# Transposing R, V and A with DMAs instead of TensorE, from the second chunk on, in a chunked recurrent-attention kernel

## The chip, the cores and the metric

The kernel runs on one core of one Trainium2 chip. The metric is the device time in microseconds (us). Three timed runs of the kernel before gave 332.66, 329.70 and 330.74 us; the median is 330.74. One execution was recorded by the hardware profiler.

## The reference

Six inputs r, k, v, w, a, b have the shape batch 4 x heads 8 x time 768 x head size 40. Each head keeps a 40 x 40 state and goes through time step by step; after that a two-layer network with a squared ReLU takes the result of all heads.

```python
for t in range(S):
    y[:, :, t] = np.einsum('bhd,bhde->bhe', rt, state)
    Sa = np.einsum('bhde,bhe->bhd', state, at)
    state_decay = state * wt[:, :, None, :] - np.einsum('bhd,bhe->bhde', Sa, bt)
    state = state_decay + np.einsum('bhd,bhe->bhde', vt, kt)
...
x = np.ascontiguousarray(attn_out.transpose(0, 2, 1, 3)).reshape(B * S, H * D)
h = x @ w_in
r = np.maximum(h, 0.0)
g = r * r
return (g @ w_out).astype(np.float32)
```

w_in is 320 x 2048 and w_out 2048 x 320; the output is 3072 x 320 in fp32.

## The kernel before

**Tiling.** Time is cut into 6 chunks of 128 steps (`L = 128`, `NCH = 6`). A unit called a batch in this document, `m` from 0 to 23, is one chunk of one batch element with all 8 heads: `m = 4 * chunk + batch element`. Within a chunk the recurrence is turned into matmuls over 128 x 128 tiles; from chunk to chunk a state (`UZ`, `UBD`) is carried. A stage `st` from 0 to 47 works on half a batch, 4 heads, so that 8 stages make a chunk; the main loop (L490) runs over the stages, with a little overhang.

**Loading.** `load(m)` (L75) issues six DMAs on the sync queue (SP), one each for W, K, B, A, V and R, of 160 KB; the tiles hold time on the partitions. Four batches may be loaded ahead. SP issues strictly in order. Beside the loads it carries `gather` (L405), eight small DMAs from SBUF to SBUF twice in a chunk that rearrange the result YS for the network, and the output rows (L460), two for each half chunk.

**Preparing a batch.** The steps are placed by a table (`when`, L470) at a stage and at one of several places, called lots, within the stage:

- `prep_cast` (L164), at stage 2m-4, lot 1: ScalarE takes the logarithm of W; GpSimd casts A, V and R to bf16 into padded tiles of 128 x 8 x 64 (two buffers each, by m % 2).
- `prep_decay` (L176), stage 2m-4, lot 4: a matmul makes the running sum of the logarithm, ScalarE the exponentials GI and G, GpSimd multiplies K and B.
- `prep_rv` (L199), stage 2m-3, lot 1: four transposes of R and four of V on TensorE (L197) into the PSUM tile t1, and one copy by ScalarE (L204) into the SBUF tile RV.
- `prep_kb` (L206), stage 2m-3, lot 4: the same for K and B.
- `prep_ga` (L214), stage 2m-2, lot 1: transposes of G and of A into the PSUM tile t3, a copy of G to GT by ScalarE (L224), and VectorE's product AT of A and GT (L225), which reads A from PSUM.
- `prep_load`, stage 2m-7, lot 5: the loads of batch m.

Each transpose handles two heads: 128 time rows by 2 x 64 columns. The tiles t1, t2, t3 share one PSUM tag of two buffers ("ff") with `cs` and with the tiles hp and op_ of the network.

**Stages.** A stage multiplies AT with KBT (`st_a_mm`, L235), masks it on VectorE (L250), goes through a short chain of corrections (P, Mc, c1, Sn: L252 to L300), transposes Sn (L310), multiplies RV (L332, which reads RV first at stage 2m+1), masks again (L349), and ends with uy (L353, L362) and YS and UZ (L373). Three pieces of the network's work (`filler`, L466) are put between the links of this chain in each stage, at the places where TensorE would otherwise sit still.

**Order.** The order is written out by hand and each engine works in program order; a wait at the head of an engine's queue holds all that is behind it. On SP each DMA also waits for the eighth DMA before it to land, because eight semaphores go round.

Of the kernel before, what the change touches and what calls it, by code (L numbers as in the profile page):

```python
# [8 lines left out]
BF16 = mybir.dt.bfloat16  # L9
I32 = mybir.dt.int32  # L10
ALU = mybir.AluOpType
# [7 lines left out]
def kernel(  # L19
# [21 lines left out]
    nc = tc.nc  # L41

    NB, NHH, T, D = r.shape
    L = 128
    NCH = T // L
    PB = NHH // 2
# [6 lines left out]
    LV = L + D  # L53
# [5 lines left out]
    gl = ctx.enter_context(tc.tile_pool(name="gl", bufs=1))  # L59
    chp = ctx.enter_context(tc.tile_pool(name="chp", bufs=2))  # L60
# [25 lines left out]
    for m in range(AHEAD):  # L86
# [11 lines left out]
        out=UTI[:], in_=ones_f[:], pattern=[[1, 128]],  # L98
# [7 lines left out]
        out=IDb[:], in_=ones_b[:], pattern=[[1, 128]],  # L106
# [3 lines left out]
    for i in range(30):  # L110
# [4 lines left out]
        out=MEX[:], in_=MEX[:], pattern=[[0, 4], [1, L]],  # L115
# [8 lines left out]
    for key, n in (("R", 2), ("V", 2), ("A", 2), ("G", 2), ("K", 4), ("B", 4)):  # L124
        pads[key] = []
        for i in range(n):
            t_ = gl.tile([128, NHH, 64], BF16, name=f"{key}p{i}")
# [3 lines left out]
    for i in range(4):  # L131
        t_ = gl.tile([128, PB, L + 2], BF16, name=f"GT{i}")
        nc.vector.memset(t_[:, :, 0:1], 1.0)
        GTs.append(t_)
        t_ = gl.tile([128, 2, PB, LV], BF16, name=f"RV{i}")
        nc.vector.memset(t_[:, :, :, L:LV], 0.0)
        for s in range(2):
            o_ = 64 * s
            nc.vector.tensor_copy(
                out=t_[o_:o_ + D, 0, :, L:LV],  # L140
                in_=IDb[o_:o_ + D, o_:o_ + D].rearrange("p (u d) -> p u d", u=1)
                .to_broadcast([D, PB, D]))
        RVs.append(t_)
    EVXs = []
    for i in range(NEV):
        t_ = gl.tile([128, 2, 2, EV], BF16, name=f"EVX{i}")
# [7 lines left out]
    def half(s):  # L154
        return slice(64 * s, 64 * s + 64)
# [3 lines left out]
    bt = {}  # L159
# [34 lines left out]
    def transposes(dst, pad):  # L194
        for j in range(PB):
            src = pad[:, 2 * j:2 * j + 2, :].rearrange("p a b -> p (a b)")
            nc.tensor.transpose(out=dst[:, j, :], in_=src, identity=IDb[:])  # L197

    def prep_rv(m):  # L199
        o = bt[m]  # L200
        t1 = ps.tile([128, 2, PB, L], BF16, name="t1", tag="ff", bufs=2)
        transposes(t1[:, 0], o.R)
        transposes(t1[:, 1], o.V)
        nc.scalar.activation(out=o.RV[:, :, :, 0:L], in_=t1[:], func=ACTF.Copy)  # L204
# [9 lines left out]
    def prep_ga(m):  # L214
        o = bt[m]
        for u in range(2):
            nc.gpsimd.tensor_copy(
                out=o.EVX[u][:, :, :, L:LV].rearrange("p i s e -> p (i s) e"),
                in_=o.V[:, 4 * u:4 * u + 4, 0:D])
        o.AT = chp.tile([128, PB, L], BF16, name="AT", tag="AT", bufs=3)  # L220
        t3 = ps.tile([128, 2, PB, L], BF16, name="t3", tag="ff", bufs=2)
        transposes(t3[:, 0], o.G)
        transposes(t3[:, 1], o.A)
        nc.scalar.activation(out=o.GT[:, :, 1:L + 1], in_=t3[:, 0], func=ACTF.Copy)  # L224
        nc.vector.tensor_tensor(out=o.AT[:], in0=t3[:, 1], in1=o.GT[:, :, 0:L], op=ALU.mult)  # L225

    def where(st):
        c, q = divmod(st, NQ)  # L230
        return c, bt[c * NB + q // 2], (q % 2) * 2, slice(2 * q, 2 * q + 2), EVXs[st % NEV]
# [3 lines left out]
    def st_a_mm(st):  # L235
        c, o, j0, p2, EVX = where(st)
        ca = CNs[st, "ps"] = [ps.tile([128, 2, 2, L], FP32, name=f"ca{s}", tag=f"ca{s}")
                              for s in range(2)]
        for u in range(2):
            for i in range(2):  # L240
                for s in range(2):
                    nc.tensor.matmul(out=ca[s][:, i, u, :], lhsT=o.KBT[half(s), u, j0 + i, :],  # L242
                                     rhs=o.AT[half(s), j0 + i, :], start=(i == 0 and u == 0),
                                     stop=True, skip_group_check=True)
# [65 lines left out]
    def st_t(st, su):  # L310
        tb = ps.tile([128, 4, 128], BF16, name="tb", tag="sp")
        if st < NS:
            EVX = EVXs[st % NEV]
            for i in range(2):
                for s in range(2):
                    nc.tensor.transpose(out=tb[half(s), i, :], in_=EVX[:, i, s, L + LV:EV],  # L316
                                        identity=IDb[:])
        if 0 <= su < NS - NQ:
            c, q = divmod(su, NQ)
            for i in range(2):  # L320
                for s in range(2):
                    nc.tensor.transpose(out=tb[half(s), 2 + i, :], identity=IDb[:],  # L322
                                        in_=UZs[(c + 1) % 2][:, 2 * q + i, half(s)])
        if st < NS:
            SnT = SnTs[st] = qdp.tile([128, 2, L], BF16, name="SnT", tag="SnT")
            nc.vector.tensor_copy(out=SnT[:], in_=tb[:, 0:2])  # L326
        if 0 <= su < NS - NQ:
            nc.scalar.activation(out=UBD[:, 2 * q:2 * q + 2, :], in_=tb[:, 2:4], func=ACTF.Copy)
# [3 lines left out]
    def st_ex_mm(st):  # L332
        c, o, j0, p2, EVX = where(st)
        SnT = SnTs.pop(st)
        ex = exs[st] = [ps.tile([128, 2, 2, L], FP32, name=f"ex{s}", tag=f"ex{s}")
                        for s in range(2)]
        for u in range(2):
            for i in range(2):
                for s in range(2):
                    lhsT = SnT[half(s), i, :] if u else o.RV[half(s), 1, j0 + i, 0:L]  # L340
                    nc.tensor.matmul(out=ex[s][:, i, u, :], lhsT=lhsT,  # L341
                                     rhs=o.RV[half(s), 0, j0 + i, 0:L],
                                     start=(i == 0 and u == 0), stop=True, skip_group_check=True)
# [9 lines left out]
    def st_z(st):  # L353
        c, o, j0, p2, EVX = where(st)
        uy = uys[st] = ps.tile([128, 2, LV], FP32, name="uy", tag="uy")
        if c > 0:
            for i in range(2):
                nc.tensor.matmul(out=uy[:, i, :], lhsT=UBD[:, p2.start + i, :],
                                 rhs=o.RV[:, 0, j0 + i, :], start=(i == 0), stop=False,
                                 skip_group_check=True)  # L360

    def st_kb(st):  # L362
# [39 lines left out]
    def load_wout():  # L402
        nc.gpsimd.dma_start(out=WOUT[:], in_=moe_w_out.rearrange("(j p) f -> p j f", p=128))
# [62 lines left out]
    def filler(st):  # L466
        if fill and fill[0][0] <= st:
            fill.pop(0)[1]()

    when = {}  # L470
    for m in range(1, NBC):
        for ds_, lot, f in ((-4, 1, prep_cast), (-4, 4, prep_decay), (-3, 1, prep_rv),
                            (-3, 4, prep_kb), (-2, 1, prep_ga), (-7, 5, prep_load)):
            if f is not prep_load or m >= AHEAD:
                when.setdefault((2 * m + ds_, lot), []).append((f, m))

    def prepare(st, lot):
        for f, m in when.pop((st, lot), []):
            f(m)
# [10 lines left out]
    for st in range(NS + 2):  # L490
        if 1 <= st <= NS:
            st_ex_mm(st - 1)
        if st + 1 < NS:
            st_a_mm(st + 1)
        filler(st)
        if st >= 2:
            st_y(st - 2)
        if 1 <= st <= NS:
            st_ex_ev(st - 1)
            st_z(st - 1)  # L500
        if st < NS:
            st_p(st)
            st_m(st)
        prepare(st, 1)
        if st < NS:
            st_corr(st, Mc[st // NQ][:, st % NQ], False)
            st_c1(st)
        if st + 1 < NS:
            st_a_ev(st + 1)
        filler(st)  # L510
        if st < NS:
            st_corr(st, c1s[st], True)
            st_sn(st)
        filler(st)
        prepare(st, 4)
        st_t(st, st - 2)
        if 1 <= st <= NS:
            st_kb(st - 1)
        if st == 1:
            load_win()  # L520
        if st == 4:
            load_wout()
        if st >= 2:
            c, q = divmod(st - 2, NQ)
            hf = q // (NQ // 2)
            if q % (NQ // 2) == NQ // 2 - 1:
                gather(c, hf, [nc.sync] if st < NS + 1 else [nc.sync, nc.gpsimd, nc.sync])
                at = st + (3 if c + 1 < NCH else 2)
                fill += [(at, lambda c=c, hf=hf, j=j: ffn_in(c, hf, j)) for j in range(NJ // 2)]
                fill += [(at, lambda c=c, hf=hf, b_=b_, p_=p_: ffn_out(c, hf, b_, p_))  # L530
                         for b_ in range(HB) for p_ in range(2)]
        prepare(st, 5)
        if st == 3:
            nc.gpsimd.memset(UZs[0][:], 0.0)
# [133 lines left out]
```

## Time and profile before

| what | value |
|---|---|
| median of three timed runs | 330.74 us (329.70 to 332.66) |
| the profiled execution's own time | 330.49 us |
| span of the profile, first to last instruction | 328.8 us |
| mean granted TensorE clock | 0.943 |
| ScalarE busy | 232.8 us (71%) |
| VectorE busy | 222.7 us (68%) |
| GpSimd busy | 188.3 us (57%) |
| transposes of R, V, A on TensorE (L197) | 96 each |
| copy of R and V out of PSUM (L204) | 24, mean 1023 ns |
| product AT (L225) | 24, mean 425 ns |

The span is what the instructions cover; the execution's own time lies 1.7 us above it. A row of a group gives busy time, mean duration of one, and the idle time ahead of it. The busy time of TensorE counts overlapping matmuls once, so that a matmul whose mean duration is 230 ns may add far less than that to it. The stages of the middle of the run are alike: a chunk takes 48.0 us (the same copy of the last Cc tile ends at 156.46, 204.43 and so on), so two batches take 24 us.

### The profile page before, as it was taken

The page shows a single profiled execution, that of the slowest core. Times are in us where ns is not written, and L with a number is a line of the kernel's source. Part 1 is how long each engine was busy: PE and PEld are TensorE (multiplying, and loading weights), DVE is VectorE, ACT ScalarE, POOL GpSimd, SP SyncE. Part 2 cuts the span into 40 slices and gives each one's busy share as a digit, 9 for nine tenths or more (in the row PEclk, how much of TensorE's full clock was granted, in tenths as well). Part 3 has the DMA queues.
Part 4 walks back from the last instruction along what each step waited for, and adds up shares of the span by engine and source line. Part 5 has one row for each costly group of instructions (what it writes and reads, how often), then busy time and mean ns, then how long its engine had stood idle before and what let it go on. Part 6 is the DMA issues. An engine that isn't in the chain of part 4 may idle for free.

```text
span 328.8 us, 10009 instructions
## 1 busy us (share of the span) xinstructions
PE 280.4 (85%) x3856; PEld 213.3 (65%) x3856; DVE 222.7 (68%) x545; ACT 232.8 (71%) x569; POOL 188.3 (57%) x342
## 2 busy tenths in 40 slices
PE   4478777799999799999799999899998899888990
PEld 3446555577777577777577777677776677666770
DVE  7226968587787587786686886686876775954430
ACT  3366766886886986887986787886887886538450
POOL 3367757296585485676476676476674673533300
PEclk9555978899999999999999999999999999999997
DMA  8992999985737437635736844735862701000100
GB/s 136 174 165 40 176 165 167 169 126 99 151 71 138 94 69 141 126 69 112 128 55 121 147 82 78 144 62 120 131 106 47 147 18 44 20 23 28 55 22 29
DMA packets 164187, 32.86 MB, mean 100 GB/s; under 512 B 158660, under 2 KB 163780, under 8 KB 164130
## 3 DMA queue, kind: packets, MB, share of 16 engines
q1 hardware_dynamic: 161586, 29.44, 49.7%
q0 software_dynamic: 2544, 2.68, 5.1%
q8 instruction: 32, 0.52, 0.7%
q14 instruction: 25, 0.20, 0.2%
HBM read 28.84 MB, written 3.93 MB: 100 GB/s over the span
## 4 chain that ended last, share of the span: by engine, by line
PE 56%; ACT 18%; issue 7%; DVE 7%; POOL 4%; DMA 3%; SPq 3%; ACTq 0%; DVEq 0%; POOLq 0%
PE hp L428 12%; PE t L197 6%; PE ex L341 4%; PE P L280 4%; PE cs L179 4%; ACT hs L433 3%; ACT jm L307 3%; PE uy L368 3%; ACT RV L204 3%; SPq L81 3%; PE tb L316 3%; PE ca L242 2%; DMA NV<-in_v_dram 2%; DVE c L288 2%; ACT GT L224 2%
## 5 line engine op out<-in xcount | busy, mean ns | idle before, releaser
L428 PE MATMUL hp<-X,WIN 120*128 120x256 bf16 (+1 forms) x576 | 78.9, 275 | 8.1 <-ACT osb L458 6.1
L433 ACT ACTIVATE hs<-hp 128x512 bf16<-128x512 f32 x96 | 57.3, 597 | 26.1 <-PE hp L428 22.7
L349 DVE TENSOR_TENSOR EVX<-ex,MEX 128x512 bf16<-128x512 f32 x96 | 61.8, 686 | 1.7 <-PE ex L341 0.5
L428 PEld LDWEIGHTS <-WIN 120*128 120x128 bf16 (+1 forms) x576 | 50.7, 98 | 18.9 <-issue 9.6
L250 DVE TENSOR_TENSOR CN<-ca,MCN 128x512 bf16<-128x512 f32 x96 | 61.4, 681 | 0.7 <-PE ca L242 0.7
L299 POOL TENSOR_TENSOR x<-Mc,c 128x160 f32<-128x160 bf16 x48 | 23.3, 486 | 66.7 <-DVE c L288 66.6
L436 POOL TENSOR_TENSOR Gt<-hs 128x512 bf16<-128x512 bf16 x43 | 48.4, 1125 | 9.9 <-ACT hs L433 9.6
L454 PEld LDWEIGHTS <-Gt 128*128 128x128 bf16 x384 | 34.3, 97 | 13.4 <-POOL Gt L436 0.8
L280 PEld LDWEIGHTS <-CN 128*128 128x128 bf16 x384 | 23.2, 98 | 27.2 <-issue 23.6
L326 DVE COPY SnT<-tb 128x256 bf16<-128x256 bf16 x48 | 14.0, 291 | 33.3 <-PE tb L322 27.6
L300 POOL TENSOR_TENSOR Cc<-x,EVX 128x160 bf16<-128x160 f32 x48 | 25.3, 527 | 17.1 <-ACT EVX L296 16.8
L436 DVE TENSOR_TENSOR Gt<-hs 128x512 bf16<-128x512 bf16 x53 | 27.4, 519 | 9.4 <-ACT hs L433 9.2
L225 DVE TENSOR_TENSOR AT<-t,GT 128x512 bf16<-128x512 bf16 x24 | 10.2, 425 | 31.4 <-ACT GT L224 31.4
L302 ACT ACTIVATE jk<-CN 128x512 bf16<-128x512 bf16 x48 | 30.1, 627 | 0.0
L212 ACT ACTIVATE KBT<-t 128x1024 bf16<-128x1024 bf16 x24 | 24.6, 1024 | 6.0 <-PE t L197 6.0
L204 ACT ACTIVATE RV<-t 128x1024 bf16<-128x1024 bf16 x24 | 24.6, 1023 | 5.1 <-PE t L197 3.0
L188 POOL TENSOR_TENSOR Kp<-NK,GI 128x320 bf16<-128x320 f32 x24 | 22.4, 933 | 6.6 <-ACT GI L182 5.6
L280 PE MATMUL P<-c,CN 128*128 128x40 bf16 x192 | 12.4, 181 | 13.5 <-DVE c L288 13.5
L288 DVE TENSOR_TENSOR c<-P,Mc 128x160 bf16<-128x160 f32 x48 | 15.3, 319 | 10.4 <-PE P L280 9.6
L378 DVE TENSOR_TENSOR YS<-uy,GT 128x256 bf16<-128x256 f32 x48 | 20.2, 421 | 1.2 <-PE uy L368 0.8
L242 PE MATMUL ca<-AT,KBT 64*128 64x128 bf16 x384 | 20.0, 228 | 1.2 <-DVE AT L225 1.2
L296 ACT ACTIVATE EVX<-P 128x160 bf16<-128x160 f32 x48 | 14.4, 300 | 8.7 <-PE P L280 8.4
(142 smaller groups left out, 636.6 us busy)
## 6 DMA issues: line engine op xcount, KB each, us to landing
NW<-in_w_dram SPq DMA_DIRECT2D x24, 160.0 KB
NK<-in_k_dram SPq DMA_DIRECT2D x24, 160.0 KB
NB<-in_b_dram SPq DMA_DIRECT2D x24, 160.0 KB
NA<-in_a_dram SPq DMA_DIRECT2D x24, 160.0 KB
NV<-in_v_dram SPq DMA_DIRECT2D x24, 160.0 KB
NR<-in_r_dram SPq DMA_DIRECT2D x24, 160.0 KB
out_dram<-osb SPq DMA_DIRECT2D x24, 160.0 KB
X<-YS SPq DMA_DIRECT2D x93, 20.0 KB
```

The lines of the kernel that those rows point to most:

```text
L204: nc.scalar.activation(out=o.RV[:, :, :, 0:L], in_=t1[:], func=ACTF.Copy)
L212: nc.scalar.activation(out=o.KBT[:], in_=t2[:], func=ACTF.Copy)
L242: nc.tensor.matmul(out=ca[s][:, i, u, :], lhsT=o.KBT[half(s), u, j0 + i, :], rhs=o.AT[half(s), j0 + i, :], start=(i == 0 and u == 0), stop ...
L250: nc.vector.tensor_tensor(out=CN[:, :, s], in0=ca[s][:], in1=MCN[:], op=ALU.mult)
L280: nc.tensor.matmul(out=P[:, i, s, 0:D], lhsT=CN[:, i, s, 1, :], rhs=X[:, 2 * i + s], start=False, stop=last, skip_group_check=True)
L300: nc.gpsimd.tensor_tensor(out=Cc[c][:, q], in0=t_[:], in1=Sn, op=ALU.add)
L302: nc.scalar.activation(out=jk[:], in_=CN[:, :, :, 1, :], func=ACTF.Square, accum_out=ACC[:, AN + st:AN + st + 1])
L349: nc.vector.tensor_tensor(out=EVX[:, :, s, 0:2 * LV].rearrange("p i (u x) -> p i u x", u=2)[:, :, :, 0:L], in0=ex[s][:], in1=MEX[:].rearra ...
L428: nc.tensor.matmul(out=hp[:, u, :], lhsT=WIN[g][0:rows[g], j * 128:(j + 1) * 128], rhs=Xs[c, hf][g][0:rows[g]].rearrange("p a b -> p (a b) ...
L433: nc.scalar.activation(out=hs[:], in_=hp[:].rearrange("p u x -> p (u x)"), func=ACTF.Relu)
L436: later.append(lambda: eng.tensor_tensor(out=Gt[:, 2 * jj:2 * jj + 2].rearrange("p j a b -> p (j a b)"), in0=hs[:], in1=hs[:], op=ALU.mult))
L454: nc.tensor.matmul(out=op_[:], lhsT=Gts[c, hf][:, j, b_, :], rhs=WOUT[:, j, :], start=(j == 0), stop=(j == NJ - 1))
```

## The change

From batch 4 on (`m >= NB`, the second chunk) the transposes of R, V and A on TensorE and the copy of R and V by ScalarE go. In their place `prep_turn` issues three transposing DMAs on the sync queue, for A, V and R in that order, each from a padded bf16 tile of 128 x 512 to an SBUF tile of 128 x 4 x 128. It stands at stage 2m-4 in a new lot 3, which is run after lot 4. A goes to a new tile AR with two buffers; V and R go straight into RV, whose rows become 8 elements longer. G, K and B are transposed on TensorE as before. The product AT reads A from AR, in SBUF. The first four batches stay as they were.

```diff
-        t_ = gl.tile([128, 2, PB, LV], BF16, name=f"RV{i}")
-        nc.vector.memset(t_[:, :, :, L:LV], 0.0)
+        t_ = gl.tile([128, 2, PB, LV + 8], BF16, name=f"RV{i}")
+        nc.vector.memset(t_[:, :, :, L:LV + 8], 0.0)
...
+    def by_dma(m):
+        return m >= NB
+
+    def prep_turn(m):
+        o = bt[m]
+        if by_dma(m):
+            o.AR = chp.tile([128, PB, L], BF16, name="AR", tag="AR")
+            for dst, pad in ((o.AR[:], o.A), (o.RV[:, 1], o.V), (o.RV[:, 0], o.R)):
+                nc.sync.dma_start_transpose(out=dst[:, :, 0:L],
+                                            in_=pad[:].rearrange("p h e -> p (h e)"))
+
     def prep_rv(m):
         o = bt[m]
+        if by_dma(m):
+            return
...
-        transposes(t3[:, 1], o.A)
+        if not by_dma(m):
+            transposes(t3[:, 1], o.A)
...
-        nc.vector.tensor_tensor(out=o.AT[:], in0=t3[:, 1], in1=o.GT[:, :, 0:L], op=ALU.mult)
+        nc.vector.tensor_tensor(out=o.AT[:], in0=o.AR[:] if by_dma(m) else t3[:, 1],
+                                in1=o.GT[:, :, 0:L], op=ALU.mult)
...
-                                 rhs=o.RV[:, 0, j0 + i, :], start=(i == 0), stop=False,
+                                 rhs=o.RV[:, 0, j0 + i, 0:LV], start=(i == 0), stop=False,
...
-        for ds_, lot, f in ((-4, 1, prep_cast), (-4, 4, prep_decay), (-3, 1, prep_rv),
+        for ds_, lot, f in ((-4, 1, prep_cast), (-4, 3, prep_turn), (-4, 4, prep_decay), (-3, 1, prep_rv),
...
         prepare(st, 4)
+        prepare(st, 3)
```

In the built program TensorE issues 240 transposes fewer (20 batches of 12, each with its weight load), ScalarE 20 copies fewer, and SP 60 DMAs more; no other engine's instructions change in number. On SP the order within two batches becomes: three transposes, two output rows, six loads, three transposes, eight gather DMAs, six loads.

## The prediction

> **What bounds the kernel now.** I read the page first, for how full each engine is, then the table by stretches, for where.
>
> ```profile
> PE 280.4 (85%) x3856; PEld 213.3 (65%) x3856; DVE 222.7 (68%) x545; ACT 232.8 (71%) x569; POOL 188.3 (57%) x342
> ```
>
> TensorE leads, but the shares are means over unlike stretches, so the table decides. Its columns: length, busy time of TensorE (PE), its weight loads, VectorE (DVE), ScalarE (ACT), GpSimd (POOL), granted clock, DMA share, GB/s.
>
> ```profile
> 20.00:62.00 42.00, 31.17 (x457) 22.91 (x455) 31.43 (x73) 29.65 (x74) 27.83 (x56) 0.78 0.86 142
> 158.00:206.00 48.00, 44.43 (x648) 34.04 (x648) 35.70 (x85) 38.52 (x98) 30.97 (x56) 1.00 0.58 105
> 254.00:300.00 46.00, 41.34 (x577) 31.16 (x577) 31.68 (x69) 31.73 (x79) 22.55 (x35) 1.00 0.21 45
> ```
>
> From 62 us on TensorE is 44.4 of 48 us busy at full granted clock: it bounds the chunk. Before that the DMA engines do (0.86). The chain of waits, 164 to 171 us (start, length, what), says the same with one addition: ScalarE's copy of R and V stands in it.
>
> ```profile
> 165.44 0.47 PE t L197 x8
> 165.91 0.02 issue
> 165.93 1.03 ACT RV L204
> 166.96 0.04 issue
> 167.00 0.82 PE hp L428 x6
> ```
>
> Eight transposes take 0.47 us there, and then TensorE's next product waits for the copy, since both use the PSUM tag "ff". Over 158 to 206 the chain gives PE t 6.7% and the copy 4.1%.
>
> The new work goes to the sync queue and the DMA engines. SP's timeline over one period of two batches:
>
> ```profile
> 158.10 0.36 SPq L460 DMA_DIRECT2D out_dram<-osb  x1
> 158.55 0.39 SPq L81 DMA_DIRECT2D NW<-in_w_dram  x1
> ...
> 162.12 0.63 SPq L81 DMA_DIRECT2D NR<-in_r_dram  x1
> 162.85 7.40 SPq L411 DMA_DIRECT2D X<-YS  x8
> 170.35 0.44 SPq L81 DMA_DIRECT2D NW<-in_w_dram  x1
> ...
> 174.52 0.89 SPq L81 DMA_DIRECT2D NR<-in_r_dram  x1
> 177.26 3.60 SPq L460 DMA_DIRECT2D out_dram<-osb  x2
> 180.96 0.40 SPq L81 DMA_DIRECT2D NW<-in_w_dram  x1
> ```
>
> SP is free only from 175.4 to 177.3, in the stretch of 3.6 us that holds two output rows, and between the two rows of the other half; it waits there for ScalarE's osb. The DMA queue over 158 to 206:
>
> ```profile
> q1 hardware_dynamic: 26976, 4.92, 57.3%
> ```
>
> So 57.3% x 24 = 13.75 us of all 16 engines go per two batches, and one packet takes 0.573 x 16 x 48 us / 26976 = 16.3 ns.
>
> **The change part by part.** The sum is made against the profiled execution, 330.5 us (span 328.8 and 1.7 around it), 0.2 below the median of 330.74.
>
> *TensorE's transposes go.* The line of the transposes alone, over the same stretch (PE, then weight loads):
>
> ```profile
> 158.00:206.00 48.00, 7.29 (x96) 5.76 (x96) 1.00 0.58 105
> ```
>
> That is 96 transposes a chunk, 76 ns each; R, V and A are half, so 3.65 us a chunk, 0.91 us a batch. *ScalarE's copy goes*: 20 x 1.02 = 20.5 us of its busy time, on the path in two of four batches (at 165.9 and at 189.1). Chain: half of PE t's 6.7% (1.6 us) and the copy's 4.1% (2.0 us) make 3.6 us a chunk. The two views agree; I take 0.91 us a batch. Of 20 batches the first two are prepared between 50 and 68 us, where the DMA share is 0.89 to 1.21, and give nothing: 18 x 0.91 = -16.4 us. Bounds: 0, if a chain of dependent work sets the stage; and 20 x (0.91 + 1.02) = -38.6, if every copy's time came back beside the transposes'.
>
> *Sixty DMAs on SP, issue.* No row shows a transposing DMA. Call its time on SP i. The nearest rows are the loads, 128 partitions like it, with medians of 0.44 to 0.84 us, and the gather, SBUF to SBUF like it, 0.77 us. I take 0.8. Lower bound 0.37 (the shortest load). Upper bound: a load moves 1024 packets; if the issue followed the number of pieces and a piece were 32 bytes (the instruction's unit is 16 rows by 128 columns, so 16 elements of 2 bytes land in a row), 131072 / 32 = 4096 pieces, 4 x 0.84 = 3.4 us. The queue's budget per two batches: loads 2 x 4.2 (158.55 to 162.75), gather 6.7, two rows 0.8, together 15.9; with 6 x 0.8 it is 20.7, and the new pace is 24 - 1.8 = 22.2. It fits, cost 0. It stops fitting at i = 1.05.
>
> *The same, on the DMA engines.* Call the time t. With 512 packets (128 partitions x 4 runs of 256 bytes) x 16.3 ns / 16 it is 0.52 us, with 4096 packets 4.2 us. I take 0.52, because the loads and gathers beside it are counted in whole runs too. 13.75 + 6 x 0.52 = 16.9 of 22.2 us: hidden. Where it isn't hidden is the DMA-bound stretch to 68 us: two batches, 6 x 0.52 = +3.1 us.
>
> A rule against the change: the Trainium skill, page "VectorE: DVE Perf Modes", section "The three transpose paths", gives 1309 ns for a 128x128 bf16 transpose by DMA and 390 ns by TensorE. The trace has 57 to 76 ns of TensorE's time apiece in the stream, and no DMA transpose. By the page, as an estimate, four in one DMA would hold the engines 5.2 us, and two batches would need 13.75 + 31.4 = 45 us: about 540 us in all. Its page "DMA: Bandwidth & Descriptors", section "Latency and other measured facts", gives 261 GB/s for transposing DMAs, 0.5 us for 128 KB, by which the sum stays as it is. No row of this trace shows which holds.
>
> *New waits.* SP's transposes wait for GpSimd's casts; the cast of R ends at 156.8 and at 171.6, and SP reaches them at 162.8 and after 175: nothing queues behind that. The buffers RV and AR were last read four and two batches earlier. Behind the transposes stand the gather and the loads. The gather ends 3i = 2.4 us later, lands 1.8 us after that (its three issues by GpSimd show 1.8), at 174.5; the first hp that reads it starts at 181.7. The second load, landing up to 4.1 us after issue (the DMA NV piece of the chain at 40.5), has the cast at 180.4 as reader: NR would land at 175.4 + 4.1 + 2.4 = 181.9 against its cast at 181.2. GpSimd idles up to 4.75 us behind the casts, which covers it; if that cover is gone, it costs 0.7 + 1.8 us per two batches, +25 us.
>
> AT is the tightest. It waits for AR, and behind it on VectorE stand c1 and the next masks, for which TensorE's corrections wait. SP reaches the second A at 162.75 + 3i + 6.7 + 5.1; issue i, landing 2.3 (1.8 + 0.52): 176.9 + 4i, 180.1 at 0.8. AT now starts at 183.9, at the new pace 181.9. So 1.8 us are left, none with a landing of 4.1.
>
> *Small edits.* AT read from SBUF: the products of two SBUF tiles of that size (Gt on VectorE) have a median of 456 ns, at least 415 and at most 1255, against 425: 20 x 0.03 = +0.6 us, -0.2 to +16.6; VectorE has 12 us free a chunk, 0. The longer RV: four memsets of 192 ns a fifth longer, in the first 7 us, beside the loads; 0. The sliced read has the same shape; 0.
>
> Sum: 330.5 - 16.4 + 3.1 = 317.2, stated as **317**.
>
> **The rivals.**
>
> *SP becomes the bound (slower).* Each 0.1 us of i beyond 1.05 costs 0.6 us per two batches; there are ten such periods, and some 6 us of lead between a landing and its reader are used up once. It eats the gain of 13.3 when 10 x (15.9 + 6i - 22.2) - 6 = 13.3, at i = 1.37. At i = 2 it gives 317 + 51 = 368 us, at 3.4 about 452. For it: SP is already busy 16 to 17 of 24 us, and the gather's 0.77 us for 20 KB shows that little data isn't a short issue. Against: no issue row has a median above 0.84.
>
> *The DMA engines become the bound (slower).* By the same sum with 13.75 + 6t they eat the gain at t = 1.73; at 4.2 it is about 475 us. [...] Against: 42% of the engines' time is free.
>
> *Hidden, and nothing gained.* If the stage's chain of P, c1, Sn, SnT sets the pace, the removed work was filler, and the time is 330.5 to 334. For it: waits such as SnT on PE tb (27.6 us in all). Against: TensorE's 44.4 of 48.
>
> *More than forecast.* If the freed "ff" buffer and ScalarE also count, up to 38.6 - 3.1 below: 295.
>
> That the change doesn't do what it says is excluded: the built program has the 240 transposes and 20 copies fewer.
>
> **How the numbers follow.** Chances: the forecast (308 to 327 as its own range: the gain from 22 down to 4) 0.45; SP the bound 0.27, because i is unmeasured and 1.05 is close to the rows (0.02 of it faster, 0.05 within 1%, 0.20 slower); the engines the bound 0.17 (0.01 within 1%, 0.16 slower); nothing gained 0.08 (0.06 and 0.02); more than forecast 0.03. Faster by over 1%, about what a measurement can tell here, 0.50; within 1% 0.12; slower 0.38. The range reaches from 308 to 368, SP's case at i = 2; about 0.05 lie below and 0.13 above.
>
> **What would show it.** Right: in 158 to 206, or its like, PE about 40.8 us a chunk, no RV row on ScalarE for later batches, a chunk of 44.4 us, SP issues of prep_turn near 0.8 us, VectorE's wait ahead of AT still ending on GT. Wrong: issues above 1.05 us and SP without gaps; AT or GpSimd's casts ended by a DMA; a DMA share near 1 past 68 us; or chunks of 48 us with PE at 40.8, which would be the chain.

## The result, and the profile after

The changed kernel takes 357.83 us (median of 4 runs, 356.40 to 361.17) against 331.05 us for the kernel before beside it: a ratio of 1.082, with a 95% interval of 1.073 to 1.091. It is slower by 8%. The forecast was 317, with 308 to 368 as the range: the time lies inside the range and on the other side of no change. The profiled execution took 361.17 us, the longest of the four, its span 359.4 us. Medians below are over all runs of a kernel; the ratios leave out the few runs that lie over 1.5% above the fastest of theirs.

First the line of busy times on the page of the kernel after, and the chain that ended last, by engine and by line.

```profile
PE 278.2 (77%) x3616; PEld 207.1 (58%) x3616; DVE 224.6 (62%) x545; ACT 215.3 (60%) x549; POOL 190.5 (53%) x342
...
PE 44%; DMA 16%; SPq 12%; issue 8%; ACT 8%; DVE 5%; POOL 4%; DVEq 0%; ACTq 0%; POOLq 0%
PE hp L443 13%; DMA AR<-Ap 12%; SPq L81 11%; PE cs L179 4%; PE P L295 4%; PE ex L356 3%; ACT hs L448 3%; PE uy L383 3%; DMA NW<-in_w_dram 3%; PE tb L331 2%; DVE c L303 2%; PE ca L257 2%; PE t L197 2%; ACT Mc L288 2%; ACT osb L473 1%
```

ScalarE lost its 17.5 us (232.8 to 215.3), as the change says. TensorE lost only 2.2 us of the 18 that 240 transposes of 76 ns make. The chain has a member that it did not have, the landing of the transposed A (12%), and one that has grown, the sync queue's issue of loads (11%, before 3%).

Two rows of the table by stretches, with the columns of the prediction's table, show the slower pace. The second has 493 matmuls where there were 648, and its granted clock, 1.00 before, is 0.97. The first has 0.88 (0.96 before), and the two stretches from 206 to 300 us have 0.89 (1.00 before).

```profile
62.00:110.00 48.00, 40.17 (x530) 30.05 (x529) 33.85 (x79) 32.73 (x84) 28.92 (x54) 0.88 0.76 128
158.00:206.00 48.00, 35.68 (x493) 26.82 (x493) 29.97 (x70) 29.93 (x79) 25.80 (x50) 0.97 0.67 113
```

TensorE now stands still for microseconds at a time, and in the stall read here it has a lower clock behind it:

```profile
204.58 0.29 PE L295 MATMUL P<-c,CN 128*128 128x40 bf16 x4 [4.38 <-DVE c L303]
```

In the single microseconds from 203 to 206 us the clock reads 0.57, 0.50 and 0.50, and it is still 0.50 up to 209 us. So a part of this stall is paid twice. For the whole run, the kernel of e9 below, which has the same matmuls, can be set beside it: TensorE is busy for 268.8 us there, at a mean clock of 0.931 against 0.892. So about 9 of the 278.2 us go with the stalls and the lower clock. That even e9 lost 11.6 us and not 18 is left open.

What the new instructions cost the sync queue is in the view of their line (shortest, median, longest duration in ns):

```profile
L207 SPq DMA_TRANSPOSE AR<-Ap x20: 1194/1394/1601, 48.3 to 303.9; - x20
L207 SPq DMA_TRANSPOSE RV<-Vp x20: 1189/1197/2325, 49.9 to 305.2; - x20
L207 SPq DMA_TRANSPOSE RV<-Rp x20: 1188/1206/2588, 51.2 to 307.6; - x20
```

None takes less than 1.19 us; I had taken 0.8. The timeline of SP over two batches of the kernel after:

```profile
177.21 1.00 SPq L475 DMA_DIRECT2D out_dram<-osb  x2
178.31 1.90 SPq L81 DMA_DIRECT2D NW<-in_w_dram  x1
...
184.07 1.47 SPq L207 DMA_TRANSPOSE AR<-Ap  x1
185.64 1.19 SPq L207 DMA_TRANSPOSE RV<-Vp  x1
186.94 1.74 SPq L207 DMA_TRANSPOSE RV<-Rp  x1
188.77 6.73 SPq L426 DMA_DIRECT2D X<-YS  x8
195.60 0.44 SPq L81 DMA_DIRECT2D NW<-in_w_dram  x1
...
198.73 2.13 SPq L81 DMA_DIRECT2D NR<-in_r_dram  x1
200.96 1.42 SPq L207 DMA_TRANSPOSE AR<-Ap  x1
...
205.08 1.00 SPq L475 DMA_DIRECT2D out_dram<-osb  x2
```

The pauses at the output rows are gone: the two rows take 1.00 us, where SP used to wait for ScalarE within 3.6 or 6.0 us. The queue is full. Over the five periods from 124.35 to 258.87 us a period of two batches takes 26.9 us: transposes 8.0, twelve loads 9.6, gather 6.7, rows 1.0, gaps between instructions 1.6. (The expectations below take 27.2.)

What the late queue does is in the chain of waits of the same stretch (start, length, what), and in the list of waits (total, times, longest):

```profile
184.07 3.42 DMA AR<-Ap
187.49 0.03 issue
187.52 0.02 DVEq L239
...
198.73 2.13 SPq L81
...
200.96 2.82 DMA AR<-Ap
```

```profile
POOL Ap L174 <- DMA NA<-in_a_dram: 44.4, 12, 6.0
...
DVE AT L239 <- DMA AR<-Ap: 37.2, 12, 5.4
```

The same in the kernel before:

```profile
DVE AT L225 <- ACT GT L224: 31.4, 24, 4.1
...
POOL Ap L174 <- DMA NA<-in_a_dram: 15.2, 4, 5.6
```

AT now waits for A's transpose, and GpSimd's casts, which the next transposes need, wait for loads that were issued late. Both are what the prediction named as tight places; each was passed.

Chunk periods are the best ruler for the experiments. Each is the distance between the starts of the last copies of Cc on ScalarE; the first number is the start of the first such copy, called the end of the first chunk here. All are in us, from one profiled execution each, and the first chunk is the least certain: in kernels without a wait for a transposed A there it ends between 58.5 and 61.4 us.

| kernel | first chunk ends | the five chunks after |
|---|---|---|
| before | 59.9 | 48.6, 48.0, 48.0, 48.0, 45.4 |
| after | 65.0 | 52.0, 53.1, 56.3, 52.0, 50.6 |
| e1 transposes beside | 60.2 | 57.7, 55.1, 52.6, 52.4, 48.9 |
| e2 V and R only | 59.9 | 50.3, 48.0, 48.6, 48.5, 45.6 |
| e3 A only | 66.1 | 47.4, 47.7, 47.7, 47.7, 45.1 |
| e5 no gather | 67.0 | 47.0, 47.5, 47.4, 47.4, 46.2 |
| e9 no transposes | 61.4 | 47.4, 47.5, 47.4, 47.5, 45.0 |
| e10 all three in one | 68.2 | 50.9, 48.2, 47.4, 47.4, 45.0 |
| e11 the same, moved | 64.4 | 48.0, 45.5, 48.3, 45.4, 43.9 |
| e12 V and R in one | 61.4 | 48.6, 47.7, 47.7, 47.7, 45.2 |
| e13 V and R in one, moved | 58.5 | 50.7, 46.3, 46.3, 46.3, 43.9 |
| e14 moves alone | 60.2 | 49.2, 48.4, 48.3, 48.3, 45.6 |
| e15 all in one, moved, later | 59.8 | 47.9, 45.3, 45.6, 47.1, 43.1 |
| e16 V and R in one, moved, later | 59.9 | 48.6, 46.3, 46.3, 46.3, 43.9 |

### The profile page after: what moved, and what is told of

The parts are those of the page before. It is cut to its first block, busy times and chain, and to the rows that moved or that the text cites. A ratio compares the mean times of both kernels' runs of the same rounds, so it can differ in the third digit from the quotient of the medians.

```text
span 359.4 us, 9675 instructions
## 1 busy us (share of the span) xinstructions
PE 278.2 (77%) x3616; PEld 207.1 (58%) x3616; DVE 224.6 (62%) x545; ACT 215.3 (60%) x549; POOL 190.5 (53%) x342
## 4 chain that ended last, share of the span: by engine, by line
PE 44%; DMA 16%; SPq 12%; issue 8%; ACT 8%; DVE 5%; POOL 4%; DVEq 0%; ACTq 0%; POOLq 0%
PE hp L443 13%; DMA AR<-Ap 12%; SPq L81 11%; PE cs L179 4%; PE P L295 4%; PE ex L356 3%; ACT hs L448 3%; PE uy L383 3%; DMA NW<-in_w_dram 3%; PE tb L331 2%; DVE c L303 2%; PE ca L257 2%; PE t L197 2%; ACT Mc L288 2%; ACT osb L473 1%
## 5 line engine op out<-in xcount | busy, mean ns | idle before, releaser
L443 PE MATMUL hp<-X,WIN 120*128 120x256 bf16 (+1 forms) x576 | 82.9, 286 | 6.1 <-ACT osb L473 6.1
L443 PEld LDWEIGHTS <-WIN 120*128 120x128 bf16 (+1 forms) x576 | 52.0, 101 | 18.0 <-issue 7.8
L265 DVE TENSOR_TENSOR CN<-ca,MCN 128x512 bf16<-128x512 f32 x96 | 61.4, 682 | 0.7 <-PE ca L257 0.7
L451 POOL TENSOR_TENSOR Gt<-hs 128x512 bf16<-128x512 bf16 x43 | 48.4, 1125 | 16.3 <-ACT hs L448 16.2
L239 DVE TENSOR_TENSOR AT<-AR,GT 128x512 bf16<-128x512 bf16 x20 | 8.5, 425 | 43.0 <-DMA AR<-Ap 37.2
L451 DVE TENSOR_TENSOR Gt<-hs 128x512 bf16<-128x512 bf16 x53 | 29.2, 552 | 9.3 <-ACT hs L448 9.2
L315 POOL TENSOR_TENSOR Cc<-x,EVX 128x160 bf16<-128x160 f32 x48 | 25.7, 535 | 17.5 <-ACT EVX L311 17.2
L174 POOL CAST Ap<-NA 128x320 bf16<-128x320 f32 x24 | 10.9, 454 | 44.4 <-DMA NA<-in_a_dram 44.4
L225 ACT ACTIVATE KBT<-t 128x1024 bf16<-128x1024 bf16 x24 | 24.6, 1024 | 7.5 <-PE t L197 7.5
L295 PE MATMUL P<-Mc,CN 128*128 128x40 bf16 x192 | 12.5, 182 | 17.0 <-ACT Mc L288 17.0
L179 PE MATMUL cs<-lnW,UTI 128*128 128x320 f32 x48 | 22.2, 552 | 1.6 <-ACT lnW L171 1.6
```

The source lines that it names most:

```text
L179: nc.tensor.matmul(out=cs[:].rearrange("p h e -> p (h e)"), lhsT=UTI[:], rhs=o.lnW[:], start=True, stop=True)
L225: nc.scalar.activation(out=o.KBT[:], in_=t2[:], func=ACTF.Copy)
L265: nc.vector.tensor_tensor(out=CN[:, :, s], in0=ca[s][:], in1=MCN[:], op=ALU.mult)
L295: nc.tensor.matmul(out=P[:, i, s, 0:D], lhsT=CN[:, i, s, 1, :], rhs=X[:, 2 * i + s], start=False, stop=last, skip_group_check=True)
L315: nc.gpsimd.tensor_tensor(out=Cc[c][:, q], in0=t_[:], in1=Sn, op=ALU.add)
L443: nc.tensor.matmul(out=hp[:, u, :], lhsT=WIN[g][0:rows[g], j * 128:(j + 1) * 128], rhs=Xs[c, hf][g][0:rows[g]].rearrange("p a b -> p (a b) ...
```

## The experiments

Three theories go through them. S: the sync queue's issue time bounds the loop. D: the DMA engines do. L, later M: the path through the landing of A and the late loads does, whatever the queue's load. Theory H came up on the way: the removed transposes had filled waits of the stage's own chain, so that TensorE's freed time was worth little from the start.

**e1, the transposes beside the old work.** In the kernel before:

```diff
+    def prep_turn(m):
+        if m >= NB:
+            J = chp.tile([128, 3, PB, L], BF16, name="J", tag="J")
+            for u, pad in ((0, o.A), (1, o.V), (2, o.R)):
+                nc.sync.dma_start_transpose(out=J[:, u], in_=pad[:].rearrange("p h e -> p (h e)"))
...
-        for ds_, lot, f in ((-4, 1, prep_cast), (-4, 4, prep_decay), (-3, 1, prep_rv),
+        for ds_, lot, f in ((-4, 1, prep_cast), (-4, 3, prep_turn), (-4, 4, prep_decay), (-3, 1, prep_rv),
...
+        prepare(st, 3)
```

> The kernel before, with the same sixty transposing DMAs issued at the same places on the sync queue but into a tile that nobody reads; TensorE and ScalarE do all that they did before. Theory S (the sync queue's issue time bounds the loop, 27 us per two batches with six transposes of 1.2 to 1.4 us in it): loads and gathers come late without any reader of the transposes, about 350 to 362 us, AT no longer waits for a DMA but GpSimd's casts do. Theory L (the loss is the landing of A's transpose, 2.8 to 3.4 us after its issue, ahead of AT): nobody waits, 330 to 334 us. Theory D (the DMA engines are full): about 345 to 362 us, with the DMA share near 1 all through.

Measured: 360.21 us, ratio 1.091 (1.086 to 1.097). The loss is there although nobody reads the transposes, and it is about that of the changed kernel. The wait moved to where S said:

```profile
POOL Ap L174 <- DMA NA<-in_a_dram: 73.8, 17, 10.1
```

L falls as the main cause: the landing of A is a victim of the late queue. D isn't told apart from S by the time of this run, though its DMA share, 0.64 to 0.79 in the four stretches from 62 to 254 us, is not the share near 1 that D asked for.

**e2 and e3, a part of the transposes.** e2: `for dst, pad in ((o.RV[:, 1], o.V), (o.RV[:, 0], o.R))`, with A on TensorE. e3: `for dst, pad in ((o.AR[:], o.A),)`, with R and V on TensorE and copied.

> The changed kernel, with A transposed on TensorE again; V and R by DMA. Theory S: the queue falls from 27.2 to 27.2 - 2 x 1.5 = 24.2 us per two batches, about 334 us plus what the early part loses, 332 to 340 us. Theory L: AT no longer waits for a DMA, so nearly the forecast gain comes back, 318 to 326 us. Theory D: 4 x 0.9 us of the engines stay, 340 to 350 us.

> The changed kernel, with R and V transposed on TensorE and copied by ScalarE again; only A by DMA, two in two batches. Theory S: the queue needs 27.2 - 4 x 1.35 = 21.8 us per two batches, less than the 24 of before, so no loss: 324 to 332 us. Theory L: AT still waits for AR, 345 to 358 us.

Measured: e2 333.65 us, ratio 1.008 (1.004 to 1.013); e3 334.74 us, ratio 1.013 (1.008 to 1.018). e2 lies where S put it. In e3 the queue has its pauses back (1.9 us for an output row) and a chunk takes 47.7 us, so S is right for the steady part. But e3 missed its range, because of a loss that S doesn't have: the first chunk ends at 66.1 instead of 59.9 us, with one wait of 5.0 us of AT for the first transposed A. In e2, where A is on TensorE, it ends at 59.9.

**e4, the gather on GpSimd.**

```diff
-                gather(c, hf, [nc.sync] if st < NS + 1 else [nc.sync, nc.gpsimd, nc.sync])
+                gather(c, hf, [nc.gpsimd] if st < NS + 1 else [nc.sync, nc.gpsimd, nc.sync])
```

> The changed kernel, with the gather DMAs issued by GpSimd, except in the last chunk as before. Theory S: the sync queue falls from 27.2 to 20.5 us per two batches and no longer bounds; GpSimd takes 16 x 0.68 = 11 us a chunk beside its 31 of 48; 318 to 330 us. Theory L: A lands somewhat earlier since half of the sets stand no longer behind a gather, 340 to 350 us. Theory D: the same bytes go through the same engines, 352 to 360 us.

Measured: 371.73 us, ratio 1.125 (1.120 to 1.130). All theories missed. The sync queue was indeed relieved: its gaps are 34 of the 140 us from 120 to 260, against 8.6 in the kernel after. But GpSimd's timeline, and then SP's timeline and its list of waits, show what the move did:

```profile
161.33 5.15 POOL L426 DMA_DIRECT2D X<-YS  x8
166.47 0.09 POOL L80 MEMSET NW<- 1x1 f32 x1
```

```profile
158.83 2.10 SPq L207 DMA_TRANSPOSE RV<-Rp  x1
166.59 0.37 SPq L81 DMA_DIRECT2D NW<-in_w_dram  x1
```

```profile
SPq L81 <- POOL NW L80: 48.8, 9, 7.7
```

The eight issues hold GpSimd for 5.15 us, and behind them in its queue stands the memset that lets the next loads go (L80). So SP sits idle from 160.9 to 166.6 and the loads come late all the same. In the kernel after, the list has 8.9 us for that wait. The run says nothing against S; it was a bad test of it.

**e5, the gather left out.** The network reads a tile of zeros, so its result is left out.

```diff
+    XC = [gl.tile([128, HB, L], BF16, name=f"XC{g}") for g in range(3)]
+    for g in range(3):
+        nc.vector.memset(XC[g][:], 0.0)
+
     def gather(c, hf, engines):
+        Xs[c, hf] = XC
+        return
```

> The changed kernel without its gather DMAs: the network reads a tile of zeros, so the network's result is left out and its work stays the same. Theory S (the sync queue's issue time): the queue falls from 27.2 to 27.2 - 8 x 0.84 = 20.5 us per two batches, below the 22.2 of TensorE's forecast pace, so the forecast gain appears: chunks of 44 to 46 us, 316 to 327 us. Theory D (the DMA engines): the gathers are 640 of some 17,000 packets in two batches, so 350 to 358 us. Theory M (the path through the landing of A and the late loads, whatever the queue's load): little changes, 345 to 358 us.

Measured: 332.57 us, ratio 1.002 (0.998 to 1.006). 25 us came back by taking 6.7 us per two batches off the queue, with next to nothing taken off the DMA engines: their share from 110 to 254 us is 0.71 to 0.77, against 0.64 to 0.70 in the changed kernel. S holds, D and M fall. But the forecast gain did not appear. Chunks take 47.4 us with the queue relieved, and 3.6 us less than 48 was the forecast. This is where H came from. (The first chunk ends late here too, at 67.0 us, with one wait of 5.6 us of AT for A.)

**e6, V and R in one DMA; e7 and e8, loads of K and B on ScalarE's queue.** The first three lines below are from the edit of e6 and e8 (the casts write into one tile of two planes), the last two are that of e7 and e8; e8 has A on TensorE.

```diff
+            nc.sync.dma_start_transpose(
+                out=o.RV[:, :, :, 0:L].rearrange("p u j x -> p (u j) x"),
+                in_=o.RVp[:].rearrange("p u h e -> p (u h e)"))
...
-            nc.sync.dma_start(
+            (nc.scalar if gate and key in "KB" else nc.sync).dma_start(
```

> The changed kernel, with V and R transposed by one DMA of twice the size (128 x 1024) instead of two; A as before. It measures what the issue time is made of. If it is a fixed cost, the large one takes 1.2 to 1.4 us, the queue falls by 2.6 us per two batches and the kernel to 335 to 345 us. If it goes with the size, it takes 2.4 us and the time stays at 355 to 360. If a fixed part of 0.4 to 0.5 us stands beside a part per piece, 1.9 to 2.0 us and 348 to 354.

> The changed kernel, with the loads of K and B (from batch 4 on) issued by ScalarE's queue. Theory S: the sync queue falls by 4 x 0.63 plus gaps, from 27.2 to 24.5 us per two batches, chunks of 49 us, 334 to 343 us; ScalarE has 5 us a chunk more to do and some 15 free. Theory D and theory M: the same transfers in the same engines, 352 to 360 us.

> V and R by one transposing DMA, A on TensorE, the loads of K and B on ScalarE's queue. Theory S: 27.2 - 2 x 1.46 (A) - 2.7 (loads) - 0 to 1.0 (merged) = 20.5 to 21.6 us per two batches: TensorE bounds again, with 64 transposes a chunk instead of 96 and no copy of R and V, chunks of 45 to 46.5 us, 317 to 325 us, faster than both kernels. Theory D: 335 to 345 us.

Measured: e6 338.54 us, ratio 1.020 (1.014 to 1.027); e7 377.01 us, 1.137 (1.131 to 1.143); e8 341.11 us, 1.028 (1.021 to 1.035). The views of the merged DMA's line in e6 (its run of 341.98 us), and of the DMAs of two and three planes in e12 and e10 below:

```profile
L217 SPq DMA_TRANSPOSE RV<-RVp x20: 1232/1238/2404, 50.9 to 284.3; - x20
```

```profile
L213 SPq DMA_TRANSPOSE RV<-RVp x20: 1258/1666/2978, 48.7 to 269.3; - x20
```

```profile
L213 SPq DMA_TRANSPOSE RV<-RVAp x20: 1446/2370/4243, 48.3 to 277.9; - x20
```

The shortest issue is 1.19 us for 128 x 512, 1.23 to 1.26 for twice that and 1.45 for three times: most of it is a fixed cost. The median of the DMA of two planes is 1.24 us in e6, where it follows A's transpose, and 1.67 in e12, where it stands right behind the loads: there it holds a wait of some 0.4 us. A in the kernel after, at the same place, has 1.39. How much of the 2.37 us of three planes is such a wait and how much is size is not shown.

e7 and e8 missed by far. ScalarE's timeline in e7 shows why:

```profile
198.20 0.38 ACTq L81 DMA_DIRECT2D NK<-in_k_dram  x1
201.85 0.38 ACTq L81 DMA_DIRECT2D NB<-in_b_dram  x1
202.32 0.60 ACT L448 ACTIVATE hs<-hp 128x512 bf16<-128x512 f32 x1 [4.48 <-DMA NK<-in_k_dram]
```

The issue itself is short. But the second load starts 3.3 us after the first has been issued, and the last row puts the wait to the landing of a DMA; all of ScalarE's work behind it waits too. ScalarE's waits for landings of K, X and W sum to 43 us in e7, and to 10 us in e8 for X and W.

**e9, no transposes of R, V and A at all.** `o.AR = ARC` (a constant tile), and no DMA in prep_turn, so the result is not the reference's.

> The changed kernel without the transposing DMAs: from batch 4 on R, V and A are neither transposed nor copied, RV keeps what the first batches left in it and A is a constant tile, so the result is not the reference's. It gives the most that the change could ever bring. The forecast's step (TensorE's busy time comes back one for one, 3.65 us a chunk): chunks of 44.4 us, 311 to 316 us. Theory H (the removed transposes filled waits of the stage's own chain, so little comes back, as the 47.4 us a chunk of the run without gathers suggest): chunks of 47 us, 323 to 329 us.

Measured: 328.51 us, ratio 0.994 (0.991 to 0.998). With the other work where it stands, this is the most that the change could bring: 0.6%, about 2 us, where the forecast had 16.4 before its costs. H holds, and the forecast's step falls. The timelines show the place. Kernel before, from the product P to its correction (L280), which needs ScalarE's copy Mc of P:

```profile
165.18 0.26 PE L264 MATMUL P<-EVX,CN 128*128 128x40 bf16 x4
...
165.29 0.38 PE L197 MATMUL t<-IDb,Rp 128*128 128x128 bf16 x4
...
165.51 0.39 PE L197 MATMUL t<-IDb,Vp 128*128 128x128 bf16 x4
165.56 0.30 ACT L273 ACTIVATE Mc<-P 128x160 bf16<-128x160 f32 x1
...
165.91 0.25 PE L280 MATMUL P<-Mc,CN 128*128 128x40 bf16 x4
```

And e9:

```profile
212.33 0.26 PE L279 MATMUL P<-EVX,CN 128*128 128x40 bf16 x4
...
212.71 0.30 ACT L288 ACTIVATE Mc<-P 128x160 bf16<-128x160 f32 x1
...
213.06 0.26 PE L295 MATMUL P<-Mc,CN 128*128 128x40 bf16 x4 [0.47 <-ACT Mc L288]
```

In both, 0.73 us lie between the start of P and the start of its correction. Before, eight transposes fill them; after, TensorE waits 0.47 us. The eight transposes cost nothing where they stood. Over the whole run, the view of the correction's line gives the idle time ahead of it, by releaser, before and in e9 ("issue" is that of its weight loads, the line of Mc that of its matmuls):

```profile
  issue: 23.6, 45
...
  ACT Mc L273: 3.9, 17
```

```profile
  issue: 37.4, 69
  ACT Mc L288: 16.4, 42
```

So TensorE's matmuls wait 12.5 us more for Mc, of the 18 us of transposes that went.

**e10, one DMA for R, V and A; e11, the same with the remaining transposes moved.** RV gets a third plane for A. e11 adds, from batch 4 on (the product AT stays at its place):

```diff
+            if by_dma(m) and f is prep_kb:
+                ds_, lot = -2, 1
+            if by_dma(m) and f is prep_ga:
+                ds_, lot = -3, 1
```

> The changed kernel, with R, V and A in one transposing DMA (128 x 1536) for each batch instead of three. Since the merged one of two took 1.24 us of the queue, as one of half its size does, theory S says: 27.2 - 4 x 1.35 = 21.8 us per two batches, the queue no longer bounds. With theory H the chunks are 47 to 47.5 us, and with the wait of the first chunk's end (5 us) 328 to 335 us; by the forecast's step 44.4 us a chunk, 316 to 323 us. If the engines' time bounds (theory D), nothing is gained over the two DMAs: 336 to 342 us.

> As the run with one DMA, and from batch 4 on G is transposed one stage earlier, where R and V were, and K and B where G and A were, with the product AT left in its place: the transposes that remain stand where the stage's chain waits for ScalarE. Theory H: the waits are filled again and chunks take 45 to 46.5 us, 320 to 328 us. Without theory H: no different from the run with one DMA, within 1%.

Measured: e10 338.25 us, ratio 1.021 (1.018 to 1.025); e11 329.00 us, ratio 0.994 (0.990 to 0.998). e10 missed its H range by 3 us: the fourth and fifth chunk take the 47.4 us expected, but the first ends at 68.2, since AT waits 7.3 us there for a DMA of three times the size, and the second and third take 50.9 and 48.2. e11 is 9 us below it by the moves alone, with two chunks of 45.4 or 45.5 us and two of 48; that is 1 us above its H range.

**e12, V and R in one DMA, A on TensorE, all loads on SP.**

> V and R by one transposing DMA, A on TensorE, all loads on the sync queue. Theory S: 27.2 - 2 x 1.46 - 2 x 1.35 = 21.6 us per two batches, the queue doesn't bound and the first chunk loses nothing: with theory H chunks of 47 to 47.5 us, 324 to 330 us; if the queue still bounds, 331 to 335 us as with two DMAs.

Measured: 330.73 us, ratio 1.000 (0.997 to 1.003). That is 0.7 us above the range for H. Chunks take 47.7 us, near what H said. The first ends at 61.4 us, as in e9, which has no transposing DMA at all, and the second takes 48.6. With the queue no longer the bound and no wait for a transposed A, the change in this form is worth nothing.

**e13 to e16, the places filled again, a control, and a later start.** e13 is e12 with the moves of e11, AT moved along with G and A. e14 is the kernel before with the same moves, R and V going where K and B were. e15 and e16 are e11 and e13 with `m >= 2 * NB`.

> V and R by one transposing DMA, A on TensorE, and from batch 4 on G and A are transposed where R and V were (one stage earlier) and K and B where G and A were. Both places in the stage's chain of waits hold eight transposes again, and only the third place, which covered nothing, is empty. Theory H: a third of TensorE's 7.3 us of transposes a chunk comes back, 2.4 us, chunks of 45.5 to 46.5 us, and no wait at the end of the first chunk: 319 to 326 us. If the places don't matter: chunks of 47.7 us as without the move, 328 to 332 us.

> A control: the kernel before, no transposing DMA, with the same moves from batch 4 on: G and A one stage earlier, K and B where G and A were, R and V where K and B were. Nothing is removed. Theory H: the same number of transposes stands in each place, so chunks of 47.5 to 48.5 us, 328 to 334 us; a gain here of over 1% would mean that the moves alone, not the DMA, make the difference.

> As the run with one DMA for R, V and A and the moved transposes, but from the third chunk on instead of the second. Theory: the wait for the first transposed A, 4.5 to 7 us at the end of the first chunk, comes from a transposing DMA that stands in the queue behind the loads of the DMA-bound start; one chunk later the engines have gaps. The loss goes and 2.5 us of one chunk's gain go with it: 323 to 328 us. If the first use costs this wherever it is: 329 to 332 us.

> As the run with V and R in one DMA and the moved transposes, but from the third chunk on. This kernel has no wait for A to lose, so a later start only gives up a chunk's gain: 1 to 3 us slower than with the start at the second chunk.

Measured: e13 324.36 us, ratio 0.981 (0.979 to 0.984); e14 331.97 us, 1.002 (1.000 to 1.004); e15 323.41 us, 0.980 (0.977 to 0.984); e16 324.03 us, 0.980 (0.977 to 0.983). So the moves alone bring nothing, the DMA alone brings nothing (e12), and both together bring 1.9%, at 46.3 us a chunk. The wait of the correction for Mc, from 110 to 254 us, is in the kernel before, in e9, in e12 and in e13:

```profile
PE P L280 <- ACT Mc L273: 1.6, 9, 0.2
```

```profile
PE P L295 <- ACT Mc L288: 9.3, 24, 0.5
```

```profile
PE P L301 <- ACT Mc L294: 6.8, 21, 0.5
```

```profile
PE P L301 <- ACT Mc L294: 1.6, 9, 0.2
```

The wait that the removal opened is closed again by the moves. The DMA share of e13 is 0.76 to 0.84 there, above that of the changed kernel, which is the second thing that speaks against D.

The later start takes 6 us off the variant with A (e11 to e15), so the first chunk's loss belongs to the DMA-bound start. e16 did not lose the 1 to 3 us expected: its second chunk takes 48.6 us, and e13's, at 50.7, had given up as much. e13, e15 and e16 are faster than both kernels, and hardly apart from each other.

## Why the prediction was wrong, point by point

**The step that failed first: "Issue", i = 0.8 us.** It measured 1.19 us at least, 1.34 us each in the steady part (8.0 / 6). The rival "SP becomes the bound" named the mechanism, and its point of decision, 1.37, is close to what was measured. But its price was off: at 1.34 its sum gives 10 x (15.9 + 8.0 - 22.2) - 6 = 11 us, so 328 and not 358. That 358 lies inside the range is therefore partly luck: the range reached to 368 by an issue time of 2 us, which was not measured. Three things were wrong. The queue's other work takes 18.9 us and not 15.9: twelve loads take 9.6 and the gaps 1.6. The fuller queue is not the reason, as the kernel before shows the same: the set of loads of 4.2 us that the prediction doubled was the shortest of the seven from 122 to 198 us, and the others took 4.9 to 5.6, gaps included (the prediction's own sum for AT has 5.1). The pace it is held against was the forecast 22.2 us, which didn't exist. And the lead of 6 us was not there: e1's chunks are long from the second on, the first with transposes all through. With these three put right, 10 x (18.9 + 8.0 - 24.0) is 29 us, near the 27 measured.

**The step that failed beside it: "TensorE's transposes go", -16.4 us.** It was mis-read, not mis-sized. The 7.29 us a chunk, of which the forecast counted half, are busy time, and busy time did not come back one for one; e9 gives 2 us of 16.4. I had two views that "agree", but both count what TensorE did and neither asks what it would have done instead. The rival "hidden, and nothing gained" was the true one for the gain and I gave it 0.08. The chain of waits could not show it: it names the transposes, because TensorE was the last to be ready, although Mc was done only 0.05 us before the correction began, the same as in e9. A chain shows what was last, not by how much.

**The DMA engines.** The number of packets was close: 32640 more, 544 for each transpose, against the 512 taken. By their sizes in the trace they are 512 of 256 bytes and 32 of 4. Their time was not right: by difference, which puts the whole of the increase on them, a transpose held the engines for (0.607 x 359.4 - 0.497 x 328.8) / 60 = 0.91 us, against 0.52 taken; that is 27 ns a packet, where 16.3 was taken. The rival's 1.73 wasn't reached, and e5 and e13 show that the engines did not bound the loop. (At 4.2 us this rival's sum gives 478 us, not 475, and the DMA share of 0.89 belongs to 44 to 50 us; neither matters here.) The engines moved 131072 bytes in those 0.91 us, that is 144 GB/s, in a queue shared with loads. From the start of the issue to the landing passed 2.7 to 3.5 us in five of the six entries of the chain between 110 and 206 us, and 4.3 in the sixth, so 1.5 us and more after an issue of 1.2, against the 2.3 after the issue that the prediction took. Of the two statements of the Trainium skill that the prediction weighed, the page "VectorE: DVE Perf Modes" (section "The three transpose paths"), with 1309 ns for one block of 128x128, read as engine time (5.2 us for the four), is far off; the page "DMA: Bandwidth & Descriptors" (section "Latency and other measured facts"), with 261 GB/s, is nearer, though the measured rate is little over half of it.

**The DMA-bound stretch, +3.1.** It was 5.2 (65.05 against 59.85), and by another way: not by the engines' time but by AT's wait of 4.4 us for one A.

**New waits.** That SP would not wait long for the casts held: from 120 to 260 us the queue stands still ahead of its 33 transposes for 4.0 us in all. The cover of the casts went, as the prediction's +25 us said it could: 44.4 us of waiting for A's load, against 15.2 before. AT, "the tightest", was late 12 times.

**Small edits.** AT from SBUF takes the same 425 ns. The memset takes 218 instead of 192 ns. Both are nothing, as said.

## What to carry to other kernels

Work that stands between two links of a dependent chain was free here up to the length of the wait; before counting its removal as a gain, look at what ends the next instruction's wait once it is gone, and plan what will stand there instead. A transposing DMA cost its queue at least 1.2 us here and little more for two or three times the size, so issue few and large ones; and before adding to an in-order DMA queue, add up its whole period, gaps and waits included, since what comes late is the load at its end. Putting DMAs on the queue of an engine that computes cost that engine their waits here (e7), and what stood behind their issue came late (e4).

## What the runs showed of the hardware that had not been expected

The issue of a transposing DMA of 128 x 512, 128 x 1024 and 128 x 1536 takes 1.19, 1.23 and 1.45 us at the shortest, against 0.37 us for the shortest load. The smallest lands 2.7 to 3.5 us after the start of its issue in the steady part, once 4.3. Behind a stall of TensorE of 4.4 us the granted clock read 0.50 for some microseconds; its busy sum was 278.2 us, against 268.8 in e9 with the same matmuls.
